# The last 384 columns of w_q's last rows, loaded by a second pair of DMAs onto 64 partitions

## The chip, the core and the metric

The kernel runs on one core of a Trainium2 chip. The core has four compute engines (TensorE for matmuls, VectorE, ScalarE, GpSimd), a sync engine (SP) that issues most of the transfers, and sixteen DMA engines that move data between HBM, the chip's main memory, and SBUF, the core's on-chip memory of 128 partitions. TensorE adds up its results in PSUM. The metric is the device time of one execution in microseconds. Before the change it is 217.96 us, the median of three runs from 217.66 to 218.02.

In the profile PE is TensorE, PEld its weight loads, DVE VectorE, ACT ScalarE, POOL GpSimd and SP the sync engine; a "q" behind such a name (SPq) is that engine's queue of DMA issues. L37 is the line of a helper that issues nearly every instruction in program order, so groups are told apart by their tiles: `kt<-ring` is an instruction that writes tile kt and reads tile ring.

## The reference

Two branches read the same input x (2 x 1 x 512), normalised over its 512 columns: attention over the last 4,096 positions of a cache, and a gated MLP whose result, through silu, multiplies the attention's. All data are float32.

```
xn = layernorm(x)                                   # (2, 1, 512)
q  = xn @ wq                                        # wq (512, 4096): 32 heads of 128
k, v = k_cache[:, :, -4096:, :], v_cache[:, :, -4096:, :]   # (2, 8 heads, 4096, 128)
p  = softmax(q @ k^T / sqrt(128))                   # 4 query heads to a key head
s  = (p @ v).reshape(2, 1, 4096) @ wo               # wo (4096, 512)
z  = gelu(xn @ w_in)                                # w_in (512, 1792)
g  = (w_sp * layernorm(z[..., 896:]) + b_sp) * z[..., :896] @ w_out   # w_out (896, 512)
out = x + s * silu(g)
```

There are two queries, so nearly all the work is reading: 64 MB of keys and values, 8 MB each of w_q and w_o, and 5 MB of w_in and w_out.

## The kernel before

**The ring.** All weights and the cache pass through one SBUF tile, `ring`, of four slots of 32 KB a partition (4 MB). A load is put into a list by `enqueue` (line 85) with the slots that it needs, and `advance` (line 92) issues loads from the head of the list on SP as soon as their slots are free. The order of loads is: w_in (slot 0), w_out (slot 1), w_q (slots 2 and 3, 8 MB), then K and V of eight units in turn (K0, K1, V0, K2, V1, ...), then w_o in three loads: 16 blocks, 8 blocks, and 8 blocks in pieces of 4, 1, 1, 1 and 1 (`load_blocks`, line 164, with the pieces in line 179). A block is one of 32 groups of 128 rows of w_o. Behind the first 16 blocks SP also issues the loads of `x4` (line 175), x laid out for the last addition, one DMA for each of the two batch rows.

**w_q.** `load_rows` (line 112) puts four consecutive rows of a weight on each partition, side by side: partition p holds rows 4p to 4p+3 of w_q, 4 x 4,096 columns, 64 KB in one piece. One DMA with 128 such rows loads it.

**Beginning.** x comes on ScalarE's queue (`xs`), is normalised to `xn`, and turned by four small TensorE transposes into `xnT` (lines 229 to 232), in which plane k holds, on partition p, the value that multiplies row 4p+k. Some constants are made on GpSimd and VectorE beside that. The MLP branch then runs: `z` (line 264) needs w_in, `y` (line 319) needs w_out. Its result is kept in `gate`.

**q.** Lines 336 to 344 multiply xn by w_q. Two PSUM banks `pq[0]` and `pq[1]` are each split into four groups of 32 partitions, and each of the eight groups takes 512 of the 4,096 columns; for each of the four planes k, eight matmuls of 512 columns run over the eight groups. A float32 matmul shows as two instructions. Line 345 frees slots 2 and 3. The results are transposed (`qT`) and spread (`qm`, `rp`, `qbd`).

**Units.** Each of the eight units (a batch row and two key heads) transposes its K on VectorE in four parts (`kt`), forms shares of the scores on TensorE (`sh`, copied to `shs`, added up in `s`), takes the maximum and the exponentials, and multiplies by V (`acc`).

**End.** Blocks 0 to 27 of w_o are multiplied into `part` (line 539), four groups of columns in turn; ScalarE copies it to `parts`. Blocks 28 to 31, the last to arrive, are multiplied into `so` in quarters (line 548), with `parts` added by `spread_quarters` ahead of block 30 (LATE, line 534). Two VectorE instructions multiply by `gate` and add `x4`, and one DMA writes the output (line 555).

**Order.** TensorE, VectorE, ScalarE and SP run their instructions in the order of the program text; GpSimd's are ordered by the compiler. All big transfers go through SP's one queue. The compiler gives each DMA one of a few semaphores, on which its readers wait.

Of the kernel before, what the change touches and what calls it, by code (L numbers as in the profile page):

```python
# [9 lines left out]
F32 = mybir.dt.float32  # L10
# [4 lines left out]
P = 128  # L15
HQ, DH = 32, 128
G = 4
# [4 lines left out]
def ap(t, offset, dims):  # L22

    return bass.AP(tensor=t.tensor, offset=t.offset + offset, ap=[list(t.ap[0])] + [list(d) for d in dims])
# [18 lines left out]
def kernel(  # L43
# [13 lines left out]
    nc = tc.nc  # L57
    pe, dve, act, sp = (InOrder(tc, e) for e in (nc.tensor, nc.vector, nc.scalar, nc.sync))
    B, _, D = x.shape
# [5 lines left out]
    KT = D // P  # L65
# [10 lines left out]
    cst = ctx.enter_context(tc.tile_pool(name="cst", bufs=1))  # L76
# [8 lines left out]
    def enqueue(load, count=1):  # L85

        at = turns[0] % 4
        turns[0] += count
        queue.append((load, range(at, at + count)))
        advance()  # L90

    def advance(*slots):
        for n in slots:
            free[n] = True
        while queue and all(free[n] for n in queue[0][1]):
            load, at = queue.pop(0)
            for n in at:
                free[n] = False
            load(ring[:, at[0] * SLOT : (at[-1] + 1) * SLOT], at[0])

    def const(name, *shape):
        return cst.tile([P, *shape], F32, tag=name, name=name)

    def bank(name, tag):
        return ps.tile([P, 512], F32, tag=tag, name=name, bufs=BANKS[tag])
# [4 lines left out]
    weight = {}  # L110

    def load_rows(name, w, k):
        def load(t, at):
            n = k * w.shape[1]
            sp.dma_start(t[:, :n], w.rearrange("(p k) f -> p (k f)", p=P))
            weight[name] = t[:, :n].rearrange("p (k f) -> p k f", k=k)

        return load

    enqueue(load_rows("in", w_in, KT))  # L120
    enqueue(load_rows("out", w_out, FT))
    enqueue(load_rows("q", wq, KT), 2)
    win, wout, wqt = (weight[n] for n in ("in", "out", "q"))

    wb1 = cst.tile([1, 2], F32, tag="wb1", name="wb1")
# [3 lines left out]
    def by_group(t):  # L129

        return bass.AP(tensor=t.tensor, offset=t.offset, ap=[[DC, G], [D, B], [1, DC]])
# [32 lines left out]
    def load_blocks(piece):  # L164
        def load(t, at):
            t = t.rearrange("p (j d) -> p j d", d=D)
            a = 0
            for n in piece:
                j = len(blocks)
                sp.dma_start(t[:, a : a + n, :], wo_v[:, j : j + n, :])  # L170
                blocks.extend((t, a + i) for i in range(n))
                a += n
            if len(blocks) == 16:
                for b in range(B):
                    sp.dma_start(x4[16 * b : P : 32, :], x[b].rearrange("o (g c) -> (o g) c", g=G))

        return load

    for piece in ((16,), (8,), (4, 1, 1, 1, 1)):
        enqueue(load_blocks(piece))  # L180


    ident = const("ident", P)
    make_identity(nc, ident)
    xnT = const("xnT", KT, 32)
    nc.gpsimd.memset(xnT, 0.0)
    ones = const("ones", P)
    nc.gpsimd.memset(ones, 1.0)
    hT = const("hT", FT, 32)
    nc.gpsimd.memset(hT, 0.0)  # L190
    x4 = const("x4", DC)
# [35 lines left out]
    xn = cst.tile([B, D], F32, tag="xn", name="xn")  # L227
    dve.tensor_scalar(xn, xs, mv[:, 0:1], rs, op0=ALU.subtract, op1=ALU.mult)
    pt = bank("xnT_ps", "sh")[:, : KT * B].rearrange("p (k b) -> p k b", k=KT)
    for k in range(KT):  # L230
        pe.transpose(pt[:, k, :], xn.rearrange("b (p k) -> b k p", k=KT)[:, k, :], ident[:B, :B])
    dve.tensor_copy(xnT[:, :, :B], pt)

    same = const("same", G, 32)
    nc.gpsimd.tensor_copy(same, ap(rowm, 0, [[0, G], [1, 32]]))
# [29 lines left out]
    for k in range(KT):  # L265
        for g in range(G):
            pe.matmul(
                pz[32 * g : 32 * g + 32, :], xnT[:, k, :], ap(win[:, k, :], g * FQ, [[FH, 2], [1, FQ]]),
                start=(k == 0), stop=(k == KT - 1),
# [50 lines left out]
    for j in range(FT):  # L320
        g = j % G
# [14 lines left out]
    pq = [bank(f"q_ps{r}", "s") for r in range(2)]  # L336
    for k in range(KT):
        for r in range(2):
            for g in range(G):
                c = (r * G + g) * 512  # L340
                pe.matmul(
                    pq[r][32 * g : 32 * g + 32, :], xnT[:, k, :], wqt[:, k, c : c + 512],
                    start=(k == 0), stop=(k == KT - 1),
                )
    advance(2, 3)
    qT = sb.tile([P, 1024], F32, tag="qT", name="qT", bufs=1)
    for r in range(2):
# [115 lines left out]
    def gather(b):  # L463

        hq = sb.tile([P, 32], F32, tag="hq", name=f"hq{b}")
        by_d = col[0][32 * b : 32 * b + 32, :].rearrange("p (j d) -> p d j", j=NCH)
        for e in range(4):
            dve.reduce_sum(hq[32 * e : 32 * e + 32, :], by_d[:, 32 * e : 32 * e + 32, :], axis=AX.X)
        t = bank(f"oT{b}", "acc")[:, :32]
        pe.matmul(t, perm, hq, start=True, stop=True)  # L470
        return t
# [56 lines left out]
    t = gather(last.b)  # L528
# [7 lines left out]
    for n in range(EARLY):  # L536
        t, a = blocks[n]
        g = n % G
# [4 lines left out]
    for n in range(EARLY, 32):  # L543
        if n == LATE:
            spread_quarters(so, parts, start=False, stop=False)
        t, a = blocks[n]
        for g in range(G):
            pe.matmul(
                so[32 * g : 32 * g + 32, :], oT[:, n, :], t[:, a, g * DC : (g + 1) * DC],
                start=(n == EARLY), stop=(n == 31),  # L550
# [33 lines left out]
```

## Time and profile before

| | us |
|---|---|
| median of three runs | 217.96 |
| lowest, highest | 217.66, 218.02 |
| the profiled execution | 218.19 |
| its span, first to last instruction | 216.4 |
| TensorE, VectorE, ScalarE, GpSimd busy | 151.1, 106.8, 43.5, 4.2 |
| bytes read from HBM | 89.40 MB |

The profile is one execution recorded by the hardware. Its span begins with the first instruction, so the execution's own time is longer by what lies before and behind (1.8 us here). A row of an engine's timeline gives the start in us, the time in us, the engine, the line, the operation, the tiles, shapes and count, and in brackets the idle time before it and what ended that. A row of stages gives the stage, its length, the busy time and instructions of each engine (PE, PEld, DVE, ACT, POOL), the granted TensorE clock, the mean busy share of the sixteen DMA engines and their GB/s. The DMA rows in 40 slices give the same share in tenths and the GB/s for 40 equal parts of a stretch. A packet is charged to the slice in which it starts. A row of a DMA queue gives packets, megabytes and their share of sixteen engines' time; besides the data, each load has one 4-byte packet for every engine that it used, which counts up its semaphore, here called a completion. Queue q1 is SP's, q10 ScalarE's, q8 and q14 fetch instructions. A row of DMA issues gives the count, KB each and the median us from issue to landing.

### The profile page before, as it was taken

The page shows a single profiled execution, that of the slowest core. Times are in us where ns is not written, and L with a number is a line of the kernel's source. Part 1 is how long each engine was busy: PE and PEld are TensorE (multiplying, and loading weights), DVE is VectorE, ACT ScalarE, POOL GpSimd, SP SyncE. Part 2 cuts the span into 40 slices and gives each one's busy share as a digit, 9 for nine tenths or more (in the row PEclk, how much of TensorE's full clock was granted, in tenths as well). Part 3 has the DMA queues.
Part 4 walks back from the last instruction along what each step waited for, and adds up shares of the span by engine and source line. Part 5 has one row for each costly group of instructions (what it writes and reads, how often), then busy time and mean ns, then how long its engine had stood idle before and what let it go on. Part 6 is the DMA issues. An engine that isn't in the chain of part 4 may idle for free.

```text
span 216.4 us, 2177 instructions
## 1 busy us (share of the span) xinstructions
PE 151.1 (70%) x848; PEld 40.3 (19%) x848; DVE 106.8 (49%) x160; ACT 43.5 (20%) x107; POOL 4.2 (2%) x22
## 2 busy tenths in 40 slices
PE   0163163933976995982997499559949946989693
PEld 0121110200211221211221132112212211223221
DVE  3305302069959269328806662793486079242201
ACT  5003310000231133042113303120421422221001
POOL 6100000000000000000000000000000000000000
PEclk9999555895796997998599769957996995899799
DMA  7999897999999999999999999999999999999980
GB/s 250 424 526 400 388 545 321 457 412 438 430 412 454 418 448 403 460 412 460 406 435 430 430 436 424 445 406 448 418 454 412 433 436 424 442 424 430 399 345 11
DMA packets 3788, 89.52 MB, mean 414 GB/s; under 512 B 434, under 2 KB 450, under 8 KB 964
## 3 DMA queue, kind: packets, MB, share of 16 engines
q1 hardware_dynamic: 3772, 89.40, 96.6%
q8 instruction: 6, 0.10, 0.2%
q14 instruction: 2, 0.02, 0.0%
q10 hardware_dynamic: 8, 0.00, 0.0%
HBM read 89.40 MB, written 0.00 MB: 413 GB/s over the span
## 4 chain that ended last, share of the span: by engine, by line
DMA 60%; PE 20%; DVE 16%; issue 1%; SPq 0%; DVEq 0%
DMA ring<-in_A_k_cache_dram 24%; DMA ring<-in_A_wo_dram 20%; DMA ring<-in_A_wq_dram 16%; DVE kt L37 12%; PE sh L37 5%; PE s L37 5%; PE q_ps L37 4%; PE acc L37 4%; PE mo L37 1%; DVE qm L37 1%; DVE qbd L37 1%; DVE m L37 1%; DVE pT L37 1%; PE col L37 0%; SPq L37 0%
## 5 line engine op out<-in xcount | busy, mean ns | idle before, releaser
L37 DVE STREAM_TRANSPOSE kt<-ring 128x2048 f32<-128x2048 f32 x32 | 72.3, 2286 | 38.6 <-DMA ring<-in_A_k_cache_dram 30.7
L37 PE MATMUL sh<-kt,qbd 128*32 128x512 f32 x256 | 42.4, 729 | 29.6 <-DVE kt L37 29.6
L37 ACT ACTIVATE shs<-sh 128x512 f32<-128x512 f32 x32 | 19.1, 597 | 121.8 <-PE sh L37 121.8
L37 PE MATMUL s<-shs,add_dq 128*128 128x512 f32 x64 | 40.3, 737 | 0.0
L37 PE MATMUL acc<-ring,pT 128*32 128x512 f32 x256 | 32.9, 642 | 0.0
L37 PEld LDWEIGHTS s<-shs,add_dq 128*128 128x128 f32 x64 | 11.3, 219 | 31.1 <-issue 26.7
L37 PEld LDWEIGHTS sh<-kt,qbd 128*32 128x32 f32 x256 | 6.5, 117 | 49.7 <-issue 40.4
L37 PEld LDWEIGHTS acc<-ring,pT 128*32 128x32 f32 x256 | 7.9, 119 | 24.6 <-issue 20.5
L37 PE MATMUL q_ps<-ring,xnT 128*32 128x512 f32 x64 | 8.6, 698 | 4.6 <-DMA ring<-in_A_wq_dram 4.6
L37 ACT ACTIVATE o<-acc,diag 128x128 f32<-128x128 f32 x30 | 8.6, 373 | 4.9 <-PE acc L37 4.9
L37 ACT ACTIVATE p<-s,nb 128x256 f32<-128x256 f32 x16 | 7.6, 487 | 6.4 <-DVE nb L37 6.2
L37 PE MATMUL part<-ring,oT 128*32 128x512 f32 x56 | 8.1, 728 | 0.8 <-DVE oT L37 0.7
L37 DVE TENSOR_REDUCE m<-s 128x2 f32<-128x512 f32 x8 | 5.3, 665 | 6.7 <-PE s L37 6.7
L37 PE MATMUL z<-ring,xnT 128*32 128x448 f32 x32 | 4.6, 727 | 5.6 <-DMA ring<-in_B_w_in_dram 5.6
L37 PE MATMUL col<-o,sel 128*32 128x512 f32 x14 | 7.3, 601 | 0.0
L37 DVE STREAM_TRANSPOSE qT<-q_ps 128x512 f32<-128x512 f32 x2 | 1.4, 717 | 10.3 <-PE q_ps L37 10.2
L37 PE MATMUL y<-ring,hT 128*32 128x512 f32 x14 | 3.6, 1060 | 3.8 <-DVE hT L37 3.8
L37 DVE STREAM_TRANSPOSE pT<-p 128x512 f32<-128x512 f32 x8 | 5.4, 674 | 1.2 <-ACT p L37 1.2
L37 ACT ACT_TABLE_LOAD x4 | 5.1, 1283 | 1.9 <-issue 1.9
L37 DVE TENSOR_TENSOR res<-so,gate 128x128 f32<-128x128 f32 x1 | 0.3, 292 | 10.3 <-PE so L37 10.3
L37 PE MATMUL xnT_ps<-ident,xn 2*128 2x2 f32 x4 | 0.6, 252 | 6.4 <-DVE xn L37 6.4
L37 DVE COPY wb<-wb_ps 128x2 f32<-128x2 f32 x1 | 0.2, 159 | 9.2 <-PE wb_ps L37 9.2
(112 smaller groups left out, 61.3 us busy)
## 6 DMA issues: line engine op xcount, KB each, us to landing
ring<-in_A_k_cache_dram SPq DMA_DIRECT2D x8, 4096.0 KB, 28.4
ring<-in_A_v_cache_dram SPq DMA_DIRECT2D x8, 4096.0 KB, 31.7
ring<-in_A_wo_dram SPq DMA_DIRECT2D x1, 4096.0 KB, 34.2
ring<-in_B_w_in_dram SPq DMA_DIRECT2D x1, 3584.0 KB, 11.7
ring<-in_A_wo_dram SPq DMA_DIRECT2D x1, 2048.0 KB, 27.4
ring<-in_B_w_out_dram SPq DMA_DIRECT2D x1, 1792.0 KB, 15.6
ring<-in_A_wo_dram SPq DMA_DIRECT2D x1, 1024.0 KB
ring<-in_A_wo_dram SPq DMA_DIRECT2D x4, 256.0 KB, 16.3
```

The costliest lines, as they stand in the source:

```text
L37: return self.tc.keep_in_program_order(call(*args, **kwargs))
```

## The change

The last 384 columns of each partition's 64 KB of w_q, that is columns 3,712 to 4,095 of the rows 4p+3, no longer come with the main load. They get a tile of their own, `wqx`, of 64 partitions with two pieces of 384 columns each. `load_q` issues two DMAs for it, one for each piece h, ahead of the main one: its source is written as 8 x 8 rows of 384 columns, so that place 8a+c of piece h takes the columns of partition 2a+16c+h; its target has 64 partitions. The main DMA then loads 16,000 of the 16,384 columns of each partition.

The same values of xn are put into the same places: `xm` on GpSimd picks them out of xn, two more transposes and a copy make `xq` from it. In the q step the last matmul of the last plane covers the 128 columns that are left of its group, and two matmuls of 384 columns over 64 partitions, one for each piece, add the rest to the same group.

Two smaller edits come with it: the two `x4` loads become one, and the last w_o load has pieces of 4, 2, 1 and 1 blocks.

```diff
-    enqueue(load_rows("q", wq, KT), 2)
+    XC = 384
+    FQL = wq.shape[1] - XC
+    wqx = cst.tile([64, 2, XC], F32, tag="wqx", name="wqx")
+
+    def load_q(t, at):
+        row = KT * wq.shape[1]
+        for h in range(2):
+            src = bass.AP(tensor=wq.tensor, offset=wq.offset + (h + 1) * row - XC, ap=[[2 * row, 8], [16 * row, 8], [1, XC]])
+            sp.dma_start(wqx[:, h, :], src)
+        n = row - XC
+        sp.dma_start(t[:, :n], bass.AP(tensor=wq.tensor, offset=wq.offset, ap=[[row, P], [1, n]]))
+        weight["q"] = t[:, :row].rearrange("p (k f) -> p k f", k=KT)
+
+    enqueue(load_q, 2)
...
-                for b in range(B):
-                    sp.dma_start(x4[16 * b : P : 32, :], x[b].rearrange("o (g c) -> (o g) c", g=G))
+                sp.dma_start(x4[0:P:16, :], by_group(x))
...
-    for piece in ((16,), (8,), (4, 1, 1, 1, 1)):
+    for piece in ((16,), (8,), (4, 2, 1, 1)):
...
+    xq = cst.tile([64, 2, 32], F32, tag="xq", name="xq")
+    nc.gpsimd.memset(xq, 0.0)
...
+    xm = cst.tile([B, 2, 64], F32, tag="xm", name="xm")
+    nc.gpsimd.tensor_copy(xm, ap(xn, KT - 1, [[KT, 2], [2 * KT, 8], [16 * KT, 8]]))
+    pt = bank("xq_ps", "sh")[:64, : 2 * B].rearrange("p (s b) -> p s b", s=2)
+    for h in range(2):
+        pe.transpose(pt[:, h, :], xm[:, h, :], ident[:B, :B])
+    dve.tensor_copy(xq[:, :, :B], pt)
...
-                pe.matmul(
-                    pq[r][32 * g : 32 * g + 32, :], xnT[:, k, :], wqt[:, k, c : c + 512],
-                    start=(k == 0), stop=(k == KT - 1),
-                )
+                n = min(512, FQL - c) if k == KT - 1 else 512
+                to = pq[r][32 * g : 32 * g + 32, :]
+                pe.matmul(to[:, :n], xnT[:, k, :], wqt[:, k, c : c + n], start=(k == 0), stop=(k == KT - 1 and n == 512))
+    for h in range(2):
+        pe.matmul(to[:, n:], xq[:, h, :], wqx[:, h, :], start=False, stop=(h == 1))
```

## The prediction

> **What bounds the kernel now.** I read the page first: the DMA rows, the queues, the chain that ended last.
>
> ```profile
> span 216.4 us, 2177 instructions
> DMA  7999897999999999999999999999999999999980
> q1 hardware_dynamic: 3772, 89.40, 96.6%
> q8 instruction: 6, 0.10, 0.2%
> q14 instruction: 2, 0.02, 0.0%
> DMA 60%; PE 20%; DVE 16%; issue 1%; SPq 0%; DVEq 0%
> L37 DVE STREAM_TRANSPOSE kt<-ring 128x2048 f32<-128x2048 f32 x32 | 72.3, 2286 | 38.6 <-DMA ring<-in_A_k_cache_dram 30.7
> ring<-in_A_k_cache_dram SPq DMA_DIRECT2D x8, 4096.0 KB, 28.4
> ```
>
> The sixteen DMA engines carry the kernel's own queue for 96.6% of the span, and the vector engine, the busiest reader of the ring, waits 30.7 us for K rows. A K load takes 28.4 us from issue to landing although its 4 MB are about 10 us of traffic at the rate below, so some two loads stand in front of it: the queue never runs dry, and a compute step that slips by a microsecond or two in the middle delays nothing. The end is set by the bytes and by how evenly they lie on the engines. Next I read the rate in the middle, and the last 12 us (0.3 us a slice).
>
> ```profile
> 60.00:180.00 120.00, 93.31 (x478) 24.08 (x474) 70.37 (x75) 28.88 (x78) 0.00 (x0) 0.87 1.00 431
> DMA  8979697998999999999755431000000000000000
> GB/s 382 410 300 546 273 492 328 410 464 348 382 416 416 410 382 355 403 382 348 280 219 212 178 137 41 27 20 14 0 0 0 0 0 0 0 0 0 14 0 0
> ```
>
> From 60 to 180 us the DMA share is 1.00 at 431 GB/s, that is 26.9 GB/s an engine. At the end the engines do not stop together. The rate is down to 219 GB/s at 210.0 (eight engines), 137 at 210.9 (five), 41 at 211.2, and from 211.5 it is 27 or less: **one engine alone** carries the last 0.8 us, to about 212.25 (half of the slice from 212.1). The other fifteen are done by about 211.35. What waits for that one engine is in the timeline of the end:
>
> ```profile
> 210.19 0.16 PEld L37 LDWEIGHTS part<-ring,oT 128*32 128x32 f32 x8 [1.02 <-DMA ring<-in_A_wo_dram]
> 210.81 0.39 PEld L37 LDWEIGHTS so<-ring,oT 128*32 128x32 f32 x8 [0.47 <-DMA ring<-in_A_wo_dram]
> 211.46 0.16 PEld L37 LDWEIGHTS so<-ring,oT 128*32 128x32 f32 x8 [0.26 <-DMA ring<-in_A_wo_dram]
> 212.03 0.16 PEld L37 LDWEIGHTS so<-parts,rowm 128*32 128x32 f32 x8 [0.41 <-ACT parts L37]
> 212.17 0.24 PEld L37 LDWEIGHTS so<-ring,oT 128*32 128x32 f32 x8
> 212.74 0.16 PEld L37 LDWEIGHTS so<-ring,oT 128*32 128x32 f32 x8 [0.34 <-DMA ring<-in_A_wo_dram]
> 213.24 0.29 DVE L37 TENSOR_TENSOR res<-so,gate 128x128 f32<-128x128 f32 x1 [10.27 <-PE so L37]
> 213.88 0.60 SPq L37 DMA_DIRECT2D out_dram<-res  x1
> ```
>
> TensorE waits for w_o blocks four times in the last 2.6 us, the last time until 212.74; from there to the end of the span are 3.7 us of fixed work. So the time follows the landing of the last engine.
>
> **Why one engine is late, and on which side it is.** No view splits the engines; the completions recorded one by one do. Each load counts one completion per engine that it used; for the 4 MB w_o load and the small x load queued behind it they are, in us:
>
> ```
> w_o, 16 blocks: 199.96 200.10 200.20 200.24 200.28 200.32 200.37 200.81 201.03 201.27 201.54 201.68 201.73 201.77 201.80 202.76
> x, b = 0:       200.43 200.55 201.22 201.45
> ```
>
> Six engines (201.54 to 202.76) lie 1.2 us or more behind the leaders, and the page has six 16 KB instruction packets in q8 that run on these engines too: one fetch each explains the six. The last is a further microsecond behind. This row (slices of 0.05 us from 1.0) shows where that may come from: the first 28 KB rows start from 1.7 on, the last engine's only at 2.6.
>
> ```profile
> GB/s 0 0 0 0 0 0 0 0 0 0 0 0 0 41 1761 574 1147 1147 573 0 573 0 0 573 0 573 0 1147 0 0 573 0 573 0 0 0 0 0 0 0
> ```
>
> [...] The x engines complete 0.2 us after their share of w_o, so all four stand among the ten earlier ones; none is in the late six. If fetches fell on any engine alike, four given engines would all be spared about one time in nine (12 over 6 by 16 over 6); if they fall on one half of the engines and x uses the other, always. I therefore put the late engine into the upper half, with 0.92.
>
> [...]
>
> **The change part by part.** (1) *384 columns off the main w_q load.* Before, every engine carried 8 of the 128 rows; 384 columns are 1,536 bytes a row, 12,288 an engine. At 26.9 GB/s that is 0.457 us less for each engine of the upper half, and as every later load queues behind, all their landings come 0.457 us sooner.
>
> (2) *The same bytes as two loads of 64 rows on the lower eight.* Each takes 16 rows of 1,536 bytes. The nearest row for short packets is the end: the lone engine needs 0.65 us (210.81 to 211.46) for its eight 2 KB packets of a block and a completion, 81 ns each against 76 by the rate, so about 5 ns lie on top. 1,536 bytes are then 57 + 5 = 62 ns, 16 of them 0.99 us, and the lower half ends 0.99 - 0.457 = 0.54 us later than now. Low bound: bytes alone, 57 ns, +0.46 us. High bound: when the queue filled up, the slowest stretch, the engines moved 287 GB/s (below), 1.5 times slower: 93 ns, +1.03 us. I take 62, by the row of nearest size.
>
> ```profile
> 2.70:4.00 1.30, 0.00 (x0) 0.00 (x0) 0.42 (x3) 1.21 (x3) 1.29 (x5) 1.00 0.67 287
> ```
>
> Cover: the lower half may be later by the lead that it has. If the latest of the fifteen (211.35) is in it, it now ends at 211.35 + 0.54 = 211.89, and the late engine at 212.25 - 0.457 = 211.79: the gain is then 0.36 us instead of 0.457. If it is an engine of the upper half, 0.457 stands.
>
> (3) *w_o pieces 4, 2, 1, 1.* One load of two blocks has 8 packets of 4 KB an engine for 16 of 2 KB: 8 x 5 ns and a completion, 0.04 us off. Block 28 now lands together with block 29. That is covered: its matmuls take 0.24 us of issue (as from 212.17), both blocks would run from 211.46 to 211.95, and the spread that follows waits for the scalar engine's copy until 212.03 anyway. Without that cover it would cost 0.24 us.
>
> (4) *SP's issues.*
>
> ```profile
> 1.63 0.48 SPq L37 DMA_DIRECT2D ring<-in_A_wq_dram  x1
> ...
> 168.93 1.23 SPq L37 DMA_DIRECT2D x<-in_A_x_dram  x2
> 180.25 22.85 SPq L37 DMA_DIRECT2D ring<-in_A_wo_dram  x6
> ...
> ring<-in_B_w_out_dram SPq DMA_DIRECT2D x1, 1792.0 KB, 15.6
> ```
>
> One x4 load for two drops an issue of 0.6 us; the next issue came 11 us later, so nothing waits. The two new issues move w_q's from 1.63 by 1.2 us (x's 0.6 each); w_in and w_out fill the queue beyond 15 us.
>
> (5) *Two more transposes, a copy on GpSimd, a copy on DVE.* They queue behind these:
>
> ```profile
> 6.38 0.61 PE L37 MATMUL xnT_ps<-ident,xn 2*128 2x2 f32 x4 [6.38 <-DVE xn L37]
> 7.02 0.17 DVE L37 COPY xnT<-xnT_ps 128x8 f32<-128x8 f32 x1 [0.79 <-PE xnT_ps L37]
> 7.34 0.29 POOL L240 COPY same_r<-rowr 128x128 f32<-128x128 f32 x1 [3.35 <-DVE rowr L37]
> 12.61 4.56 PE L37 MATMUL z<-ring,xnT 128*32 128x448 f32 x32 [5.62 <-DMA ring<-in_B_w_in_dram]
> ```
>
> A GpSimd copy of 0.3, two transposes of 0.15 and a copy of 0.2 end near 8 us; behind them on TensorE is only z, idle for 5.62 us until w_in lands. Cost nothing.
>
> (6) *The split last column group and two matmuls over wqx.*
>
> ```profile
> 36.15 8.60 PE L37 MATMUL q_ps<-ring,xnT 128*32 128x512 f32 x64 [4.64 <-DMA ring<-in_A_wq_dram]
> 44.82 0.54 SPq L37 DMA_DIRECT2D ring<-in_A_k_cache_dram  x1
> ...
> 58.27 0.53 SPq L37 DMA_DIRECT2D ring<-in_A_v_cache_dram  x1
> ...
> L37 PE MATMUL q_ps<-ring,xnT x64: 592/592/1061, 36.1 to 44.2; 128*32 128x512 f32 x64
> ```
>
> Before, four column groups run beside each other, a pass of 512 columns in 0.59 us; the two new matmuls run alone on one group, four passes (two each) of 0.59 x 384/512 = 0.44 us, at most 1.8 us. The q phase ends up to 2 us later, and so do the K load at 44.82 and the V load at 58.27; both stand 20 us and more ahead of their landing (28.4 for K). Cost nothing; without that queue, 2 us.
>
> **Sum.** 0.457 + 0.04 = 0.50 us off. The profiled execution is 218.19 us around its span of 216.4; it would become 217.69. The median of the runs is 217.96, 0.23 below it; with the same step it becomes **217.46**. By the bounds the gain runs from -0.09 (93 ns, latest engine below: 211.35 + 1.03 - 0.04 = 212.34 against 212.25) to 0.50.
>
> **Rivals.** *The small rows cost so much that the lower half becomes last.* The place is the moment between w_out and w_q; with the latest of the fifteen in that half it decides from 87 ns a row (211.35 - 0.50 + 16 x 0.087 = 212.25). For it: an engine's eight rows of one load lie 1 MB apart in w_q, and the load writes to half of the partitions alone, which no large load of before does. At double the cost, 124 ns, the end is 212.83: slower by 0.58, 218.54. Against: the 2 KB rows, also scattered, cost only 5 ns extra. [...]
>
> *The late engine is in the lower half.* It gets +0.54 - 0.04: 218.46. Against it stand the x completions.
>
> *The load is sprayed over sixteen engines after all.* Each gives and takes 12,288 bytes; 8 x 5 ns more, 0.04 less: 217.96, no change.
>
> *The fetches fall otherwise.* With a dozen more TensorE instructions a fetch may come elsewhere. If the last engine is spared its fetch, the second of the upper half (201.80, 0.96 earlier) is no limit and the lower half decides: if its latest stopped at 210.9, the end is 210.9 + 0.54 - 0.04 = 211.40, 0.85 sooner: 217.1. If a fetch strikes a lower engine that ended at 211.35, it ends 1.2 later than 211.89: 218.8.
>
> **How the numbers follow.** Forecast 0.68 (own range 217.3 to 217.7, by 0.40 (0.36 + 0.04) to 0.50 off and 0.15 of run spread); small rows 0.14, anywhere from 217.6 to 218.54; lower half 0.07; sixteen engines 0.05; fetches 0.06. A measurement tells about 0.2%, 0.44 us, from no change, and the forecast lies just beyond it: of its 0.68 I count 0.48 faster and 0.20 same. Of the small rows' 0.14, 0.06 same and 0.08 slower; the lower half is slower (0.07); sixteen engines same (0.05); of the fetches 0.04 faster, 0.02 slower. Together 0.52, 0.31 and 0.17. The range 217.1 to 218.4 leaves out the lower half, the upper end of the small rows and part of the fetches, under 0.2.
>
> **What would show it.** The last 12 us by slices: the stretch with one engine at 27 GB/s shrinks from 0.8 us to near nothing, and the last wait of TensorE for w_o ends at 212.25 instead of 212.74. q1 counts 3,768 packets with eight engines (3,772, plus 128 rows and 16 completions, less 4 completions of x, 128 rows and 16 completions of the merged blocks) and 3,784 with sixteen. q_ps ends 1 to 2 us later with no later K landing. It is wrong if the lone tail is longer than before (lower half), equal (sixteen engines), or if eight engines end together late (small rows).

## The result and the profile after

The change made the kernel slower. The median of six runs is 219.03 us (218.52 to 219.29), against 218.01 us (217.66 to 218.43) for the kernel before beside it: a ratio of 1.0044, with a 95% interval of 1.0028 to 1.0060. That is 1.0 us more where 0.5 us less was forecast, and it lies above the predicted range. The profiled execution took 218.92 us.

The page of the kernel after shows the same bound as before, and the packet count that was forecast for eight engines:

```profile
span 216.9 us, 2193 instructions
DMA  7999999999999999999999999999999999999990
q1 hardware_dynamic: 3768, 89.40, 96.7%
q8 instruction: 7, 0.11, 0.2%
q14 instruction: 3, 0.02, 0.0%
```

The end of the kernel after, as the DMA rows of 204 to 217 us (40 slices of 0.325 us) and as the timeline, answers to the two fences that the prediction shows for before:

```profile
DMA  9899797989899999999987521100010000000000
GB/s 655 353 454 454 328 504 328 429 378 403 366 378 429 416 378 416 416 397 366 353 334 290 221 95 76 44 19 0 0 50 0 0 0 0 0 11 2 0 0 0
```

```profile
210.71 0.16 PEld L37 LDWEIGHTS part<-ring,oT 128*32 128x32 f32 x8 [1.47 <-DMA ring<-in_A_wo_dram]
211.97 0.38 PEld L37 LDWEIGHTS so<-ring,oT 128*32 128x32 f32 x16 [1.10 <-DMA ring<-in_A_wo_dram]
212.56 0.16 PEld L37 LDWEIGHTS so<-parts,rowm 128*32 128x32 f32 x8 [0.21 <-ACT parts L37]
213.23 0.16 PEld L37 LDWEIGHTS so<-ring,oT 128*32 128x32 f32 x8 [0.30 <-DMA ring<-in_A_wo_dram]
213.73 0.29 DVE L37 TENSOR_TENSOR res<-so,gate 128x128 f32<-128x128 f32 x1 [11.30 <-PE so L37]
```

Two things are to be seen. The engines stop more closely together: before, the last slices with data (0.3 us each) held 41, 27, 20 and 14 GB/s, one engine alone for 0.8 us; now they (0.325 us each) hold 76, 44 and 19, one alone for about 0.4 us (the 50 further on is an instruction packet, the one of q8 in this stretch). But all of it comes later: the share leaves nine tenths at 210.5 instead of 209.7, and TensorE's last wait for w_o ends at 213.23 instead of 212.74. The balance was improved, and the whole queue was delayed by more than that was worth.

The stretch from 16 to 18 us, first of before and then of after, shows a slower queue early in the kernel. Before, a DMA share of 1.06 goes with 459 GB/s (a share above 1 is possible because a packet is charged to the stretch in which it starts), that is 433 GB/s for a full share; after, 0.92 goes with 307, that is 334:

```profile
16.00:18.00 2.00, 1.48 (x18) 0.43 (x6) 0.35 (x2) 0.54 (x1) 0.00 (x0) 1.00 1.06 459
16.00:18.00 2.00, 2.00 (x17) 0.28 (x8) 0.00 (x0) 0.00 (x0) 0.00 (x0) 1.00 0.92 307
```

Where the delay enters is in the single packet records, which no view of the profile lists. They have a start, a time and a size, and no engine. In us (starts) and ns (times), the first row of the main w_q load on each of the sixteen engines:

```
before: starts 15.12 to 16.39, 65,536-byte rows of 2,418 (of all 128, two take 2,420 and 2,435)
after:  starts 15.23 to 15.74, eight engines: 64,000-byte rows of 3,055 to 3,061
        starts 16.55 to 17.45, eight engines: 2,593 to 2,815 (one 3,008), a mean of 2,764
        later rows, all engines: 2,361 to 2,373
wqx rows of 1,536 bytes: the first 32 take 65 each; the last 96 have a mean of 102; all 128 a mean of 93
```

The eight engines that start w_q first, at 15.23 to 15.74, can have carried no packet of `wqx`: sixteen of its rows take at least 16 x 65 ns = 1.04 us, and the first starts at 15.25. They are the upper half, as the lower half is the eight engines of the `wqx` loads (each load has eight completions), and while the lower half loads `wqx` they too are slow: 3,058 - 2,361 = 0.70 us lost, where 0.457 us was to be gained. The lower engines pay 16 rows of 93 ns, 1.49 us, and 0.40 us in the mean on the first main row. Over the sixteen engines the first main rows cost 0.55 us more than the later ones and the short rows 0.74; less the 0.457 us of bytes that left the main rows, that is 0.83 us. The completions of the 4 MB w_o load near 200 us show nearly this: their mean goes from 200.99 to 201.87, by 0.88 us. Their last goes from 202.76 to 203.28, so the distance from the mean to the last shrank from 1.77 to 1.41. The four engines of the x load, which the author took to be among the lower eight, show the larger delay that this half has: their completions have a mean of 202.40, against 200.91 and 201.09 for the two x loads of before, 1.31 to 1.49 us more.

The two profiled spans differ by only 0.5 us (216.4 and 216.9). The profiled execution of before was a late one: 23 executions of the same kernel beside a later experiment have a median span of 215.9 (215.5 to 216.1). The six of the kernel after have a median of 217.0 (216.5 to 217.3), so the loss of span is rather 1.1 us. The rows account for 0.83 of it; the experiments with 16 columns below lose 0.4 us with no slow short row, and what makes that is open.

### The profile page after: what moved, and what is told of

Its sections match the earlier page's. It is cut to its first block, busy times and chain, and to the rows that moved or that the text cites. A ratio compares the mean times of both kernels' runs of the same rounds, so it can differ in the third digit from the quotient of the medians.

```text
span 216.9 us, 2193 instructions
## 1 busy us (share of the span) xinstructions
PE 150.1 (69%) x854; PEld 40.8 (19%) x854; DVE 107.1 (49%) x161; ACT 43.5 (20%) x107; POOL 4.7 (2%) x24
## 3 DMA queue, kind: packets, MB, share of 16 engines
q1 hardware_dynamic: 3768, 89.40, 96.7%
## 4 chain that ended last, share of the span: by engine, by line
DMA 48%; PE 30%; DVE 18%; issue 1%; SPq 1%; DVEq 0%
DMA ring<-in_A_k_cache_dram 24%; DMA ring<-in_A_wq_dram 16%; DVE kt L37 13%; PE sh L37 9%; PE s L37 8%; DMA ring<-in_A_wo_dram 8%; PE acc L37 5%; PE q_ps L37 5%; SPq L37 1%; PE mo L37 1%; PE so L37 1%; PE col L37 1%; DVE qm L37 1%; DVE qbd L37 1%; DVE m L37 1%
## 5 line engine op out<-in xcount | busy, mean ns | idle before, releaser
L37 PE MATMUL sh<-kt,qbd 128*32 128x512 f32 x256 | 43.2, 733 | 29.2 <-DVE kt L37 29.2
L37 PE MATMUL s<-shs,add_dq 128*128 128x512 f32 x64 | 39.3, 721 | 0.0
L37 PE MATMUL acc<-ring,pT 128*32 128x512 f32 x256 | 30.5, 602 | 0.0
L37 PE MATMUL q_ps<-ring,xnT 128*32 128x512 f32 (+1 forms) x64 | 9.3, 735 | 4.7 <-DMA ring<-in_A_wq_dram 4.7
L37 PE MATMUL z<-ring,xnT 128*32 128x448 f32 x32 | 5.9, 920 | 5.0 <-DMA ring<-in_B_w_in_dram 5.0
L37 PE MATMUL part<-ring,oT 128*32 128x512 f32 x56 | 6.6, 597 | 3.3 <-DMA ring<-in_A_wo_dram 3.3
## 6 DMA issues: line engine op xcount, KB each, us to landing
ring<-in_B_w_out_dram SPq DMA_DIRECT2D x1, 1792.0 KB, 15.7
```

The source lines that it names most:

```text
L37: return self.tc.keep_in_program_order(call(*args, **kwargs))
```

## The experiments

Each kernel starts from the kernel after unless it says otherwise, and each was run beside the kernel before, whose median is given with it. Three theories stood at first: the short rows are slow because of their source (rows 1 MB apart), because of the shape of the target (64 partitions), or because half of the engines run alone.

**The two parts alone.** One kernel has the split without the two small edits (the lines under its name, against the kernel after). The other is the kernel before with the small edits alone; against the kernel after its load of w_q changes back (the lines under its name), and the preparation of `xq` and the two matmuls over `wqx` are left out.

```diff
# e1_split_only
-                sp.dma_start(x4[0:P:16, :], by_group(x))
+                for b in range(B):
+                    sp.dma_start(x4[16 * b : P : 32, :], x[b].rearrange("o (g c) -> (o g) c", g=G))
-    for piece in ((16,), (8,), (4, 2, 1, 1)):
+    for piece in ((16,), (8,), (4, 1, 1, 1, 1)):
# e2_tail_only
-    enqueue(load_q, 2)
+    enqueue(load_rows("q", wq, KT), 2)
```

> The w_q split as in the change, without the two small edits (two x4 loads, pieces 4, 1, 1, 1, 1 as before). If the loss of 1.0 us (218.01 to 219.03) comes from the split, this run is at 218.9 to 219.1 and its first 64,000-byte rows of w_q take about 3.06 us on eight engines, as in the changed kernel, against 2.42 us for 65,536 bytes before. If it comes from the small edits, it is at 217.5 to 218.0.

> Before, with the two small edits alone (one x4 load, pieces 4, 2, 1, 1). If the split is the cause: 217.9 to 218.1, no change. If the edits at the end are: 218.5 to 219.0, with the last wait for w_o longer than before.

Before: 217.66 us. The split alone took 219.42 (218.52 to 220.46), ratio 1.0074 [1.0049, 1.0099]; the small edits alone 217.76 (217.39 to 217.95), ratio 0.9997 [0.9983, 1.0011]. The whole loss is the split's. The small edits gain nothing that can be measured. The profiled execution of their kernel is the fastest of its twelve, and shows an end of the unchanged w_q without the late engine:

```profile
DMA  9697989999999999975533000000000000000000
...
211.83 0.16 PEld L37 LDWEIGHTS so<-ring,oT 128*32 128x32 f32 x8 [0.32 <-DMA ring<-in_A_wo_dram]
```

No engine is alone at this end. The share steps from nine tenths to five and to three; the last landings, read from the completions of the last w_o load, are 211.53 to 211.79 for six engines (its page counts six packets of 16 KB in q8) and 210.98 for the latest of the others. So the lead that the change could even out is 0.81 us here, where the profile of before had one engine 0.9 us behind all others (212.25 against 211.35); bytes taken from one half go to the other, so half of it, 0.4 us, is the most that it is worth.

**The loads taken away.** `wqx` is filled with zeros instead, so the product leaves out these columns of the rows 4p+3; all else stays, the two added matmuls too.

```diff
-            src = bass.AP(tensor=wq.tensor, ...)
-            sp.dma_start(wqx[:, h, :], src)
+            nc.gpsimd.memset(wqx[:, h, :], 0.0)
```

> The changed kernel without the two wqx loads: wqx is filled with zeros, so the last 384 columns of row 4p+3 are left out of the product. It bounds what the loads cost: every engine carries 12,288 bytes less. Theory (the loads slow all engines): the first 64,000-byte rows take 2.36 us and the time is 217.4 to 217.6, 0.457 us under before, so the loads cost 1.5 us. Rival (64,000-byte rows or the two added matmuls are the cost): the first rows stay slow, or the end is at 218.5 and more.

217.34 us (217.24 to 218.63), ratio 0.9990 [0.9974, 1.0006]. In its trace the first main rows take 2,361 ns like the later ones (one of them 2,453). The start of the q step, which waits for the last row of w_q, moves with it; these are the timeline rows of TensorE for the kernel after, for e2 and for e4:

```profile
37.08 4.50 PE L37 MATMUL q_ps<-ring,xnT 128*32 128x512 f32 x20 [4.66 <-DMA ring<-in_A_wq_dram]
```

```profile
35.44 5.73 PE L37 MATMUL q_ps<-ring,xnT 128*32 128x512 f32 x28 [3.73 <-DMA ring<-in_A_wq_dram]
```

```profile
34.94 6.57 PE L37 MATMUL q_ps<-ring,xnT 128*32 128x512 f32 x32 [2.99 <-DMA ring<-in_A_wq_dram]
```

With the loads TensorE's wait for the last of w_q ends 2.1 us later than without them (37.08 and 34.94). Sixteen rows at 65 ns would be 1.04; the rest is the slowing. The median span is 215.3 us against 215.8 for before, which is the 0.457 us of bytes that here no engine carries any more; 0.2 us of it are lost outside the span (the last experiment).

**The source.** The loads read one contiguous block of w_q, other numbers than the product needs; target and bytes stay. Each load then ran on sixteen engines, as its 16 completions show, so this run also tells whether the eight engines matter.

```diff
-    ap=[[2 * row, 8], [16 * row, 8], [1, XC]]
+    ap=[[8 * XC, 8], [XC, 8], [1, XC]]      # offset h * 64 * XC
```

> The changed kernel, but the two wqx loads read their 64 rows of 1,536 bytes side by side from the start of w_q instead of from the ends of 128 rows that lie 64 KB apart; targets, sizes and engines are the same, the last 384 columns of the product are other numbers. Theory: reads 64 KB and 1 MB apart meet in one part of HBM and slow all sixteen engines; then here the first 64,000-byte rows take 2.36 us, the 1,536-byte rows about 65 ns, and the time is 217.4 to 218.0. Rival: the short rows themselves, or their writing to half of the partitions, are slow; then the first rows stay at about 3.06 us, the short rows at 90 to 130 ns, and the time at 218.9 to 219.1.

218.87 us (218.63 to 218.92), ratio 1.0047 [1.0031, 1.0062]. Short rows go from 65 to a mean of 100 ns for the last 96, the first main rows take 2,652 to 3,141. Neither the pitch of the source nor the use of eight engines makes the slowness. What stays the same is the target of 64 partitions, and rows of 1,536 bytes.

**The target.** Two kernels change the target. In e5 four loads fill 32 partitions each, and the inner step of the source is 512 KB instead of 1 MB. The author meant each of the eight engines to write a group of four partitions by itself; no record shows which engine wrote which. In e6 one load fills 128 partitions on sixteen engines, and the preparation of `xq` is left out, since the rows of this load lie on the partitions as the values of `xnT` do.

```diff
# e5_own_port
-    wqx = cst.tile([64, 2, XC], F32, tag="wqx", name="wqx")
+    wqx = cst.tile([32, 4, XC], F32, tag="wqx", name="wqx")
-        for h in range(2):
-            ... ap=[[2 * row, 8], [16 * row, 8], [1, XC]]
+        for h in range(4):
+            ... ap=[[row, 8], [8 * row, 4], [1, XC]]
# e6_sixteen
+    wqx = cst.tile([128, XC], F32, tag="wqx", name="wqx")
+        sp.dma_start(wqx, ... ap=[[row, P], [1, XC]])
```

> [...] Theory A (two engines that write into the same group of partitions get in each other's way, and the other engines wait with them): the 1,536-byte rows take 65 ns throughout, the first 64,000-byte rows 2.36 to 2.45 us, and the time is 217.4 to 217.9. Theory B (the short rows on half of the engines are slow wherever they are written): the short rows stay at 90 to 130 ns, the first rows at about 3 us, and the time at 218.7 to 219.2. [...]

> The last 384 columns as one load of 128 rows of 1,536 bytes on 128 partitions and all sixteen engines, one matmul over 128 partitions, no xq; nothing is moved between engines. Theory A: every engine writes its usual partitions, so the short rows take about 62 ns and nothing slows: 217.7 to 217.9 (beside 217.7 before). Theory B: the short rows are slow in themselves, 90 ns and more, with slow first rows of the main load: 218.2 to 218.6.

Before: 217.84 us. In both traces all 128 short rows take 65 ns, and the first main rows 2,361 like the later ones (one of 2,509 in e5). The stretch from 16 to 18 us of e5 has 523 GB/s at a share of 1.23, that is 425 GB/s for a full share, near the 433 of before:

```profile
16.00:18.00 2.00, 1.60 (x14) 0.43 (x6) 0.23 (x2) 0.54 (x1) 0.00 (x0) 1.00 1.23 523
```

e6 took 217.81 (217.51 to 218.02), ratio 0.9996 [0.9983, 1.0010]: no change, as the rival with sixteen engines had it. In e5 the profiled execution took 217.71, but the median is 218.45 (217.66 to 218.99), ratio 1.0019 [1.0003, 1.0035]. Its spans fall into two groups, four of 215.6 to 215.8 and eight of 216.3 to 216.9; the trace is from the lower group. So the slowing of the rows is gone in this trace, and something else is there in most executions.

**Bytes or rows.** One load of 64 rows of 3,072 bytes: half the number of rows, the same bytes, from other columns of w_q than the product needs.

```diff
-        for h in range(2): ...
+        src = bass.AP(..., ap=[[2 * row, 8], [16 * row, 8], [1, 2 * XC]])
+        sp.dma_start(wqx.rearrange("p h c -> p (h c)"), src)
```

> The changed kernel with one load of 64 rows of 3,072 bytes for the two of 64 rows of 1,536: the same bytes on the same engines and partitions, half as many rows (other columns of w_q, so the last 384 columns of the product are other numbers). Theory A (bytes written across the engines' partition groups): the rows take twice as long, about 200 ns, the first main rows stay at about 3 us, time 218.7 to 219.1. Theory B (a cost for each short row): the loss halves, 218.2 to 218.5, and the first main rows take 2.7 us or less.

219.98 us (219.18 to 221.66), ratio 1.0104 [1.0068, 1.0141], before 217.84: the slowest of all. The first 19 rows take 121 ns; the mean of all 64 is 185, the highest 373, and the first main rows of the upper engines take 3,273 to 3,279. With half of the rows the cost did not fall, so it is not a price for each row.

**Four partitions further on.** As e5, but the target is partitions 4 to 35 instead of 0 to 31. The author meant each engine to write, again by itself, another group than in the loads beside it; that is not shown either. `wqx` is zeroed on GpSimd first, and the matmuls read partitions 0 to 31, so the product has other numbers.

> [...] If two engines on one group are the cause, the short rows stay at 65 ns, the first main rows at 2.36 us, and the time is 217.7 to 218.6 as with partitions 0 to 31. If writing outside its own group is enough to slow an engine, the short rows take 90 ns and more, and the time is 218.7 to 219.3.

Before: 217.78 us. 219.11 us (218.82 to 219.31), ratio 1.0051 [1.0033, 1.0069]. Rows stay at 65 ns until 15.9 us and then take 65 to 138; the first main rows of the upper engines take 2,784 to 2,831. As far as the loads go, this is e5 but for four partitions, with the same source. The rows and the time are those of the expectation's second theory, but as no record has an engine's partitions, the run shows no more than that these four partitions matter. The onset doesn't single out a cause: until 15.96 some engine still has a row of w_out, and nothing is slow before 15.90, when the eight engines of the load have yet to begin their main rows (16.18).

**Another place.** In e15 the two loads go behind the main w_q load, in e16 the four loads of e5 do.

```diff
+        n = row - XC
+        sp.dma_start(t[:, :n], bass.AP(...))
         for h in range(2):                  # e16: range(4), 32 partitions
             sp.dma_start(wqx[:, h, :], src)
-        n = row - XC
-        sp.dma_start(t[:, :n], bass.AP(...))
```

> The changed kernel with the two wqx loads issued behind the main load of w_q, so that they run beside K0 at about 34 us instead of beside w_q at 15 us. If the writes to 64 partitions slow whatever runs beside them, the first main rows of w_q take 2.36 us, the 1,536-byte rows 90 to 130 ns, eight 32 KB rows of K0 take 1.7 to 2 us instead of 1.21, and the time is again 218.7 to 219.3. If the slowing belongs to the start of w_q, the time is 217.6 to 218.0.

> The four 32-partition loads of 384 columns go behind the main w_q load instead of ahead of it. In the kernels with four loads ahead, SP issued the main load only at 11.9 to 12.3 us, behind a wait of 7.2 us for w_in; here it should go out near 1.6 us. If that late issue costs the 0.4 to 0.6 us of span that most executions of those kernels lose, the times fall to 217.6 to 217.9 with none above 218.2. If the loss belongs to the four loads or to the balance itself, the times stay at 218.3 to 218.5 in most executions.

e15 took 219.51 us (219.19 to 220.40), ratio 1.0086 [1.0061, 1.0111], before 217.89. The first main rows of w_q all take 2,361 ns, the short rows again mostly 65 and then a mean of 101, and now the first 32 KB rows of K0 are hit: 1,506 to 2,044 ns instead of 1,213. The slowing follows the loads wherever they stand. e16 has the same place and none of it: short rows 65, K0 rows 1,213. Its q step starts 1.15 us sooner than e15's:

```profile
36.38 5.11 PE L37 MATMUL q_ps<-ring,xnT 128*32 128x512 f32 x24 [4.17 <-DMA ring<-in_A_wq_dram]
```

```profile
35.23 6.23 PE L37 MATMUL q_ps<-ring,xnT 128*32 128x512 f32 x44 [2.94 <-DMA ring<-in_A_wq_dram]
```

Yet e16's median is 218.42 (217.48 to 218.84), ratio 1.0024 [1.0012, 1.0036], before 217.78; its profiled execution has a span of 215.7 and the other eleven 215.9 to 217.0.

**The rest that e5 still loses.** Does it go with the bytes moved, and does it repeat? e9 is e5 with 192 columns, e11 and e12 are e9 again, e14 is e5 with 16 columns, which moves next to nothing, and e17 is e14 with the loads behind the main one.

> The variant with targets of 32 partitions, with 192 columns instead of 384: half of the bytes are moved. With 384 columns nothing is slowed, and yet its median is 218.45 beside 217.84: the lower half, given 16 x 65 ns = 1.04 us less 0.457, now ends last as often as not. Theory: with 192 columns the upper half gains 0.23 us and the lower loses 16 x 37 - 228 = 0.36 us, which its lead of some 0.6 us covers: 217.6 to 217.9, the 0.2 us outside the span included, no clear gain. Rival (the split itself costs, whatever it moves): 218.2 and more.

> The 192-column variant with targets of 32 partitions once more, for its trace: of its twelve runs three are at 217.8 to 218.1 (the profiled one is 217.92) and nine at 218.3 to 218.6. Theory: in the second group one engine of the lower half, which now carries more, is hit by an instruction fetch or starts late and ends about 0.6 us after all others; the w_o completions then show one last straggler that belongs to that half. Rival: all sixteen engines are later by 0.6 us, that is, something slows the stream as a whole.

> The same kernel a second time, since one run can fall into either group: the same two readings.

> The variant with targets of 32 partitions and only 16 columns: four loads on eight engines that move next to nothing (64 bytes a row). The variants with 384 and 192 columns slow no row in their traces, and yet most of their runs have a span of about 216.5 us beside 215.9 before, whatever the bytes moved. If it is the moved bytes, the span here is at 215.7 to 216.0 and the time, with 0.2 us more outside the span, at 217.7 to 218.0. If four more loads, or the added instructions, are enough, the span stays at 216.3 to 216.6 and the time at 218.3 to 218.6.

> The same order with 16 columns, so that next to nothing is moved to the eight engines. By the late issue: 217.8 to 218.0, that is before plus the 0.2 us outside the span. By the four loads or the added instructions themselves: 218.3 as with the loads ahead.

e9 missed what its theory gave (217.6 to 217.9) and came out as the rival had it: 218.51 us (217.84 to 218.58), ratio 1.0022 [1.0009, 1.0034], before 217.78, though in its trace all short rows take 36 ns. e11 and e12, one execution each, gave 217.96 and 217.91 with spans of 215.9, again the lower group. e14 took 218.34 (217.99 to 218.51), ratio 1.0012 [0.9996, 1.0027], before 217.89, with spans of 216.0 to 216.5 beside a median of 215.9 for before: nearly the same loss of span without the bytes. Its profiled execution, with a span of 216.2, is a usual one. Its completions of the 4 MB w_o load have a mean of 201.10, like those of e5 (201.05), but the last two come at 202.33 and 202.40 and the third last at 201.83, where the last of e5 is 201.71. So here two engines are late, and not the whole stream; which, and why, the records don't say. One suspect was SP's queue. With four loads ahead, SP issues the main w_q load only after a wait for w_in; this is e5, and then e16, in which it goes first:

```profile
1.64 3.00 SPq L37 DMA_DIRECT2D wqx<-in_A_wq_dram  x4
11.86 0.33 SPq L37 DMA_DIRECT2D ring<-in_A_wq_dram  x1
```

```profile
1.62 0.48 SPq L37 DMA_DIRECT2D ring<-in_A_wq_dram  x1
2.15 10.52 SPq L37 DMA_DIRECT2D wqx<-in_A_wq_dram  x4
```

e17 has the early issue too and took 218.12 (217.62 to 218.37), ratio 1.0015 [1.0006, 1.0024], before 217.78, with a median span of 216.3, like e14's. The late issue is not the cause of the span; the four loads, or the instructions that go with them, are, and by what way stays open. e4 and e7 (below) have such instructions, two transposes where these have four, without the loads, and their spans (medians 215.3 and 215.9) are no longer than before's (215.8 and 215.9): that points at the loads and does not prove it.

**The preparation alone.** The kernel before, with the copies, transposes and memset for `xq` that nothing reads.

> Before, with the preparation of xq alone (memset, copy on GpSimd, two transposes, copy on VectorE), which nothing reads. Theory: hidden before w_in lands, the span stays at that of before; the time outside the span, 1.8 us before (218.19 - 216.4) and 2.0 us in all kernels with the split (218.92 - 216.9, 217.33 - 215.3), shows whether these instructions bring the 0.2 us: time 217.6 to 217.9. Rival: the preparation delays the start or the constants: 218.2 and more.

217.93 us (217.62 to 218.91), ratio 1.0007 [0.9991, 1.0023], before 217.84. The spans are as before (215.6 to 216.3), but the time outside the span is 2.03 us in the median instead of 1.81. The kernel after has 2.01. e2 and e6, without this preparation, have 1.81; e16 and e17, which have it, have 1.81 and 1.83. So 0.2 us outside the span goes with some of these programs, and the instructions by themselves don't explain it.

## Why the prediction was wrong

**The step that failed is (2), the price of the moved rows and whom it hits.** It said 62 ns a row, at most 93 ns, paid by the lower half alone: "the lower half ends 0.99 - 0.457 = 0.54 us later than now". Measured: a mean of 93 ns, 1.49 us for sixteen, a mean of 0.40 us more on the first main row of the lower engines, and 0.70 us on the first main row of the upper eight. By the working of that step the upper half is then 0.70 - 0.457 = 0.24 us later instead of 0.457 sooner, and the lower about 1.4 us (1.49 + 0.40 - 0.457) instead of 0.54. The sum 0.50 fell with it. The high bound of 93 ns was met by the mean; what was left out, at nothing and without a reason, is that a load on eight engines can slow the main rows of all sixteen.

The cause that the runs leave is the target, which partitions the load writes. Shown, in one trace each: with targets of 32 partitions from 0 (e5, e9, e16) and of 128 (e6) a row costs 65 ns (36 for 768 bytes) and the rows beside it keep their time but for a few, while a target of 64 partitions (after, e1, e3, e8, e15) or one of 32 from partition 4 on (e10) slows the short rows and the rows of all sixteen engines beside them. It isn't the pitch of the source (e3), the number of engines (e3 and e6 both use sixteen) or of rows (e8), or the place in the queue (e15). Not shown is which engine wrote which partition, and so in what way the target does this: no record has it. The theory of two engines on one group of partitions was the author's, and the runs neither show nor exclude it. The late rows of after take up to 182 ns, with a mean of 106 from the first slow one on. That the upper engines, which have no packet of `wqx`, are slowed too is measured (3,055 to 3,061 ns against 2,361); in what way is not shown.

**The gain was oversized as well.** The prediction read the lead of the lower half from one trace with one very late engine. That engine's late start at 2.6 us is not the reason that it was taken for: in e5 the last engine starts at 2.80, and the last three completions lie within 0.1 us of each other. Step (1)'s 0.457 us less for each upper engine holds row by row (2,418 - 2,361 = 57 ns, eight times 0.457). But at the end of e2, even with short rows of 65 ns, the lower half would land 16 x 0.065 - 0.457 = 0.58 us later, at 211.56, and the upper at 211.33: 0.2 us sooner than 211.79, by this estimate. e16, in whose trace no row is slowed, shows some evening out and no gain: the distance from the mean to the last completion of the 4 MB w_o load is 0.78 us (201.04 to 201.82) against 0.99 in e2 (200.87 to 201.86), and the span of its best execution is 215.7 against 215.6 for e2's. In e5 the distance is 0.66, and in e6, which moves nothing between the halves, 0.98.

**"Cost nothing", step (5), holds for the span; for the whole it is open.** The instructions lie where they were put, and z waits 5 us for w_in behind them:

```profile
6.33 0.40 POOL L250 COPY xm<-xn 2x128 f32<-2x128 f32 x1 [2.25 <-DVE xn L37]
6.89 0.24 PE L37 MATMUL xq_ps<-ident,xm 2*64 2x2 f32 x2
7.24 0.15 DVE L37 COPY xq<-xq_ps 64x4 f32<-64x4 f32 x1
12.11 1.72 PE L37 MATMUL z<-ring,xnT 128*32 128x448 f32 x8 [4.97 <-DMA ring<-in_B_w_in_dram]
```

But e7, e4 and the kernel after have 0.2 us more outside the span, while e16 and e17 have the instructions and not the 0.2 us; for this the prediction had no term.

**Right were** the eight engines (3,768 packets, eight completions a load) and, as far as single traces tell, the late half: taking bytes from the upper half and giving them to the lower shrank the distance from the mean to the last completion in e5 and e16. That the late engines are those with the instruction fetches is not shown, as no record has the engine of a packet. Nor does any record number the engines: that x's four are among the lower eight, on which the choice of the halves in (1) and (2) rests, was the author's assumption, and no run shows it outright. What the trace of after shows is eight completions for each `wqx` load and x's delay of 1.31 to 1.49 us, near the 1.4 of the lower half and far from the 0.24 of the upper. The small edits (3) and (4) brought no loss (e2), and the 0.04 us of (3) is below what can be told. (6) holds: e4 has the added matmuls and a median span 0.5 us below before's. The q step ends later, and the K part that VectorE waits for first behind it is there at the same time.

```profile
46.27 1.48 PE L37 MATMUL q_ps<-wqx,xq 64*32 64x384 f32 x4
46.42 0.54 SPq L37 DMA_DIRECT2D ring<-in_A_k_cache_dram  x1
...
61.23 0.54 SPq L37 DMA_DIRECT2D ring<-in_A_v_cache_dram  x1
...
76.67 2.31 DVE L37 STREAM_TRANSPOSE kt<-ring 128x2048 f32<-128x2048 f32 x1 [2.52 <-DMA ring<-in_A_k_cache_dram]
```

```profile
76.69 2.31 DVE L37 STREAM_TRANSPOSE kt<-ring 128x2048 f32<-128x2048 f32 x1 [5.20 <-DMA ring<-in_A_k_cache_dram]
```

The first fence is after, the second before. The K issue comes 1.6 us later (46.42 against 44.82) and the V issue 3 us later (61.23 against 58.27); the first K part that VectorE waits for behind them is there at 76.67 and 76.69. Only VectorE's own wait got shorter, from 5.20 to 2.52 us.

**The rival that came nearest** is the one of small rows, with 0.14: it had the place, between w_out and w_q, and slower as the sign. Of its two reasons the source rows 1 MB apart fell with e3 (which rows an engine takes is in no record); the other, a load that writes to half of the partitions alone, is what the runs point at. Its picture, eight engines late together, is not what the end shows: all sixteen are late and end more closely together than before.

## What to carry to other kernels

Before a load is given to fewer engines or fewer partitions, ask which partitions it will write and what else is written at that time, and time it on another target; here the same bytes on eight engines cost 65 ns a row or up to 138 by a target four partitions further on (e5 and e10), up to 182 with 64 partitions, and they slowed engines that carried none of them. A lead that one trace shows at the end is to be checked against several executions before it is spent: here the last landing of the profile was 0.9 us later than in the trace of e2. When a balance of 0.4 us at most is to be had, added loads can cost as much by themselves, as e14 does.

## What was not expected of the hardware

- Eight engines slow the other eight: rows of 64,000 bytes on engines without a packet of the load take 3,055 to 3,061 ns instead of 2,361 in the kernel after, and 3,273 to 3,279 in e8.
- The first rows of a slow load (43 of 128 in the kernel after, 58 in e1, 61 in e10, 83 in e3) run at full speed, 65 ns, and the slowing sets in behind them, at 15.7 to 15.9 us in all four.
- A contiguous source of 8 x 8 rows to the same target ran on sixteen engines, where the strided one ran on eight (e3, 16 completions against 8).
- In e5 SP issued its seventh load only when w_in had landed, behind a wait of 7.2 us (issue at 11.86 us instead of 3.11 in the kernel after); its w_q rows started at 15.19 as in before (15.12), so this cost nothing there.
- Kernels with four 32-partition loads have executions of two kinds: in e5 and e16 most spans lie 0.7 to 1.3 us above that of the profiled execution, in e9 mostly 0.4 to 0.7, and no trace tells why.
